# A hand-written order of 968 operations, changed: Pool's list begins with loads, DVE clears the sinks' value tile, and each engine's operations move by a few places

## The chip, the core and the metric

The kernel runs on one core of one Trainium2 chip. A core has five engines that run side by side and wait for each other by semaphores: PE (TensorE, matrix multiply), ACT (ScalarE), DVE (VectorE), POOL (GpSimd) and SP (SyncE, which here only issues DMAs). Sixteen DMA engines move data. POOL's DMAs go through one queue, SP's and ACT's through others. The metric is the time of one launch in device microseconds; less is better.

## The reference

Attention with a sliding window and a few sink keys, then a two-layer perceptron with a sigmoid-gated middle:

```python
q, k, v: (4, 8, 768, 64)      # batch, heads, positions, head width
scores = q @ k.T / sqrt(64)
keep = (pos_k < 4) | ((0 <= pos_q - pos_k) & (pos_q - pos_k < 128))
a = softmax(where(keep, scores, -1e9))
x = (a @ v) as (3072, 512)    # tokens x (heads * width)
h = x @ w_in                  # w_in (512, 2048)
g = h * 1 / (1 + exp(-1.702 * h))
out = g @ w_out               # w_out (2048, 512)
```

## The kernel before

**Tiles.** The 4 x 768 query positions are cut into 24 blocks of 128. Block b is position b % 6 of batch b // 6. A block needs the keys and values of itself and of the block before it in its batch, and the four sink keys of the batch. Blocks 0, 6, 12 and 18 begin a batch and need only themselves; they are done first, then 1, 2, 3, 4, 5, 7 and so on.

**One block's steps, by their names in the code:**
- `q`, `k`, `v` (lines 271, 310, 318): Pool issues a DMA that loads a block and converts it to 16 bits. 128 KB each. Pool also issues the eight weight loads `wi0..3` and `wo0..3` (lines 324 and 331, 512 KB each).
- `tq`, `tk` (383): PE transposes q and k of the first eight blocks through PSUM; `cq`, `ck` are the copies out of it, on ACT or DVE. Later blocks are transposed in pairs by a DMA that SP issues, `tqk` (429).
- `msk` (464), `sc` (478, 483): PE writes the mask and the scores. `snk` (507) are the scores of the sinks.
- `pk`, `mx`, `ms`, `sb`, `ssb` (535 to 596, DVE): the window's two triangles are packed into one tile, the row maximum taken and subtracted; blocks 0, 6, 12 and 18 have `nb` in place of the subtraction.
- `bx`, `ex` (568, 606, ACT): the exponential.
- `ta` (650, PE) with its copy `ca`, or from the seventh block on `tat` (681, a DMA transpose that SP issues): the weights are transposed into tile `at`.
- `sp`, `so` (637, POOL): two selects split the packed triangles again into `atp` (previous block) and `at` (own block).
- `av` (705 to 712, PE): the product with the values, in two halves `av7_0`, `av7_1`. The first matmul (705) adds the sinks through the tile `vsb`; the others are 710 and 712.
- `nm` (722, 723, DVE): division by the sum, into `xn`. `tx` and `cx` (740), or the DMA transpose `txd` (753): `xn` transposed into `xT`.

**The perceptron.** Groups of one or two blocks: g0 is block 0, g1 block 6, g2 blocks 12 and 18, then pairs. `h7_3` is step 3 of the first layer of group 7 (786, PE), `th` and `g` are its gate (800, 807, 816), `o9_1` is step 1 of the four of the second layer for block 9 (836, PE), `ev` the copy out of PSUM (245 on ACT, 239 and 241 on DVE), `st` the store that SP issues (856). A group's first-layer steps use `xT` of all its blocks.

**The sinks' value tile.** `vsa` holds the sink values of each batch (four small DMAs on SP, line 339), with ones beside them. `vsb` (128 x 2080 elements of 16 bits) must be zero but for 32 rows; operation `zv` (228) clears it, and `vsb0..3` (344) write into it the product of `vsa` and an owner mask `own`, one batch each.

**The order.** All operations are recorded in a list of 968; each has an engine or a choice of engines. The string `ORDER` names all of them by number, and a letter after a number (d, a, p, s) chooses DVE, ACT, POOL or SP where there is a choice. They are emitted in that order, so an engine's instruction list is the subsequence of its own operations, and each engine works its list strictly in order. `Plan.emit` asserts that an operation comes behind all that it needs; waits between engines are put in from data and buffers by the framework. Buffers come from rings (three PSUM tiles tagged `mm` for all transposes and both layers, two for scores, four output tiles), so that a buffer's next user waits for its last one. Pool's DMAs use eight completion semaphores in turn: the ninth load is issued only when the first has landed, and so on. Loads of later blocks also depend on the selects of the block six places earlier (line 766).

```python
z_v = plan.add("zv", {DVE: 0.65, POOL: 1.8}, 0,
    lambda e: (nc.vector if e == DVE else nc.gpsimd).memset(vsb, 0.0), key=-880)
for word in order.split():
    choice = letter.get(word[-1])
    op = self.ops[int(word[:-1] if choice else word)]
    op.emit(choice) if len(op.eng) > 1 else op.emit()
```

Of the kernel before, what the change touches and what calls it, by code (L numbers as in the profile page):

```python
# [52 lines left out]


ORDER = """
1a 9 4s 10 11 8p 100 12 2a 7 6 13 0a 94 5a 98 3a 15 96 14 23 107 17 21 101d 26 104 95d 105a 20 102 99d 29 103a 171 97d
108 18 172a 125 106 16 109 150 126a 112 19 194 151a 110 195a 113 148 27 111 149d 225 24 226d 127 114 88 115 152 128d
92 116a 130 129 90 117 119 131 118a 120 86 196 132 121 173 87 197a 122 174a 22 133 135 123 134 199 175 89 124d 138 136
200 25 137 613 139d 30 142 614 153 143 140 615 154 141a 91 619 155 158 144 620 156 145 157 159 621 146 93 616 147d 160
637 617 634 638 618 32 176 639 635 631 636 177 632 610 178 36 633 161 611 179 35 181 628 162a 612 180 163 182 165 622  # L60
164d 166 183 184 33 167 623 185d 629 168 28 198 630 188 204 34 169 640 201 170a 205 227 641 228a 189 39 186 206 624
187a 202 209 230 642 231 203 215 190 38 207 643 208 216d 191 210 217 229 644a 43 192 235 645 211 193a 625 232 31 212a
236 280 37 282 626a 256 233 258 283a 627 652 41 259a 281d 234 257a 649 213 653 238 237 40 261 241 661 650 654 214 239
262 260 651 42 662 285 242 263 304 240 655 218 243a 286 663 44 219 656 646 266 45 657 658 647 220 244 664 648 659 46
267 670 665 245 660 221 671 264 222 246 672 247a 269 265 248 250 268 667 249 666 270 284 251 49 676 668 271 290 47 669
252 677 287 48 253 323 673 288 254 674a 678 291 255a 675 289 306 223 679 292 224a 293 682 307 272 294 680d 305 683 681
688 273 311 295 308 684 50 312 689 686 51 685 309 692 52 313 687 310 276 693 690 314 277 315 704 344 324 345 705 330
691 316 327 325 694 326 331 274 695 296 696 275 361 328 698 697 297 332 278 699 279a 329 53 298 333 334 343 54 299 700
346 317 349 300 701 347 55 335 706 301 702a 318 350 302 703 707 303a 348 57 716 351 399 708a 58 352 362 353 56 709 319
365 717 712 354 368 336 720 320 713 321 337 722 721 322 714 59 723 363 61 718 715 364 366 60 340 719 710 369 724 367  # L70
711 371 370 726 725 341 372 732 338 733 355 339 381 342 382 356 384 727 387 734 64 373 383 388 728 63 385 419 735 62
389 359 736a 390 729 386 737 360 391 750 374 730d 742 392 751 375 752 731 401 67 400 743 402 738 753 406 65 403 378 66
739 746 407 379 748 747 404 376 749 740 408 377 744 741 405 357 409 745 420 358 410 754 393 423 380 426 439 760 440
394 421 755 411 422 68 424 761 427 70 457 756 425 69 762 429 428 757 430 412 766 758d 431 438 413 767 772 444 759 441
72 397 763 445 773 73 442 768 764a 71 398 770 765 769 443 495 416 446 771 788 447 417 448 780 414 458 415 432 774 461
781 449 464 459 433 789 460 462 395 775 74 778 396 75 776 465 418 779 76 463 436 777 782 466 437 790 467 468 783 791
450 784 792d 469 451 434 785 435 78 793 802 786a 514 79 800 803 77 454 798 787 455 470 801 476 799 794 482 471 479 452
795 808 453 80 796 456 809 81 477 806 797 478 82 480 804 807 483 474 805 816 481 475 810 484 497 817 485 498 486 496
516 502 818 499 811 487 503 822 500 552 812 504 823 501 819 505 517 813 820d 506 488 472 821 814d 824 473 489 815 836
825 507 535 83 515 536 828 518 85 837 521 492 84 829 834 519 493 826 835 522 490 827 508 830 520 491 832 831 509 523  # L80
494 844 524 833 525 534 845 590 537 540 838 538 526 846 541 839 539 542 864 543 544 840 512 865 545 527 553 513 847
556 528 559 573 841 848a 574 849 510 842a 852 511 843 546 860 853 529 861 547 850 530 854 851 554 866 855 555 557 531
856 532 560 858 533 857 558 867 859 562 561 550 872 563 551 862 592 868 593 863 564 591 873 597 594 548 880 598 595
869 881 599 565 888 870a 600 596 874 871 889 566 549 601 886 875 567 876d 572 887 602 568 882 575 569 877 578 883 884
570 892 579 571 885 576 878 893 603 580 890 879 581 577 604 894 891 582 900 895 912 583 901 913 607 902 608 896 910
584 897 911 916 585 898a 605 899 917 914 606 918 915 908 919 586 909 906 587 903 907 588 904a 922 589 905 920 609 923
921 928 924 929 925 930 926a 948 927 931 949 938 932a 940 933 939 936 941 946 937 934 947 942 935 950 943 956 944 957
945 951 958 952 962 953 963 954a 959 964 955 960a 965 961 966a 967
"""


# [807 lines left out]
```

## Time and profile before

| | |
|---|---|
| median of three runs | 234.69 us (233.06 to 235.38) |
| the profiled execution, its own time | 235.79 us |
| its span, first to last instruction | 234.10 us |
| granted TensorE clock | 1.00 throughout |
| DMA moved | 32.07 MB, mean 137 GB/s |
| Pool's DMA queue, share of 16 engines' time | 71.9% |
| the queue of SP's and ACT's DMAs | 39.7% |

Durations below come from the profiled execution, which ran 1.1 us longer than the median. PE rows are single matmuls or merged ones, and their ends are modelled. PEld is PE's loading of weights, which runs beside the matmuls. In an instruction's row the bracket at the end gives how long the engine stood idle before it and what ended that.

### The profile page before, as it was taken

The page shows a single profiled execution, that of the slowest core. Times are in us where ns is not written, and L with a number is a line of the kernel's source. Part 1 is how long each engine was busy: PE and PEld are TensorE (multiplying, and loading weights), DVE is VectorE, ACT ScalarE, POOL GpSimd, SP SyncE. Part 2 cuts the span into 40 slices and gives each one's busy share as a digit, 9 for nine tenths or more (in the row PEclk, how much of TensorE's full clock was granted, in tenths as well). Part 3 has the DMA queues.
Part 4 walks back from the last instruction along what each step waited for, and adds up shares of the span by engine and source line. Part 5 has one row for each costly group of instructions (what it writes and reads, how often), then busy time and mean ns, then how long its engine had stood idle before and what let it go on. Part 6 is the DMA issues. An engine that isn't in the chain of part 4 may idle for free.

```text
span 234.1 us, 5451 instructions
## 1 busy us (share of the span) xinstructions
PE 217.5 (93%) x2202; PEld 151.3 (65%) x2202; DVE 150.2 (64%) x384; ACT 143.6 (61%) x224; POOL 111.7 (48%) x129
## 2 busy tenths in 40 slices
PE   1588889999999998979999989999999999999994
PEld 0476765685586585567577567576577676675863
DVE  3478688899978858859787427779647883120000
ACT  2387774874498686266378564697566687552632
POOL 8884344995378729449187294083340303300000
PEclk9999999999999999999999999999999999999999
DMA  3999999999999999999999999999632343313202
GB/s 53 180 159 206 201 196 185 180 170 111 150 226 149 145 219 111 114 234 118 171 221 125 173 171 178 120 194 131 120 115 48 69 97 72 68 42 78 92 0 90
DMA packets 120904, 32.07 MB, mean 137 GB/s; under 512 B 112016, under 2 KB 117936, under 8 KB 120880
## 3 DMA queue, kind: packets, MB, share of 16 engines
q0 software_dynamic: 69888, 13.64, 71.9%
q1 hardware_dynamic: 50272, 17.96, 39.7%
q8 instruction: 17, 0.28, 0.5%
q10 hardware_dynamic: 720, 0.13, 0.3%
q14 instruction: 7, 0.06, 0.1%
HBM read 27.46 MB, written 6.29 MB: 144 GB/s over the span
## 4 chain that ended last, share of the span: by engine, by line
PE 67%; DMA 22%; DVE 5%; POOL 4%; issue 1%; ACT 1%; SPq 0%; POOLq 0%
PE o L836 29%; PE hT L786 27%; DMA w_out<-in_moe_w_out_dram 7%; DMA at<-a 6%; PE sc L483 3%; DMA xT<-xn 3%; DMA v<-in_v_dram 3%; DMA qkn<-in_k_dram 2%; PE av L710 2%; PE av L712 2%; PE av L705 1%; DVE sc L535 1%; POOL at L637 1%; POOL atp L637 1%; DVE mx L545 1%; POOL vsb L228 1%
## 5 line engine op out<-in xcount | busy, mean ns | idle before, releaser
L786 PE MATMUL hT<-xT,w_in 128*128 128x256 f16 (+1 forms) x832 | 94.0, 264 | 1.9 <-DMA xT<-xn 0.9
L836 PE MATMUL o<-w_out,gT 128*128 128x512 f16 (+2 forms) x400 | 92.6, 371 | 0.7 <-DMA w_out<-in_moe_w_out_dram 0.7
L786 PEld LDWEIGHTS <-w_in 128*128 128x128 f16 x832 | 73.8, 98 | 15.9 <-issue 3.7
L816 ACT ACTIVATE gT<-hT 128x512 f16<-128x512 f32 x80 | 46.1, 597 | 28.8 <-PE hT L786 28.3
L637 POOL TENSOR_SCALAR_AFFINE_SELECT atp<-at 128x1024 f16<-128x1024 f16 (+1 forms) x22 | 22.4, 1017 | 74.6 <-DMA at<-a 61.2
L836 PEld LDWEIGHTS <-gT 128*128 128x128 f16 x400 | 35.8, 97 | 33.2 <-issue 2.2
L545 DVE TENSOR_REDUCE mx<-sc 128x4 f32<-128x512 f32 x48 | 32.6, 683 | 1.7 <-PE sc L478 1.7
L535 DVE COPY_PREDICATED sc<-later,sc 128x512 f32<-128x512 uint16 x40 | 26.0, 691 | 7.4 <-PE sc L483 7.1
L606 ACT ACTIVATE a<-e 128x1056 f16<-128x1056 f32 (+2 forms) x24 | 22.3, 935 | 8.7 <-issue 5.8
L582 DVE TENSOR_TENSOR e<-sc,mx 128x512 f32<-128x512 f32 x40 | 26.5, 682 | 0.0
L722 DVE RECIPROCAL rcp<-av 128x4 f32<-128x4 f32 x48 | 8.5, 177 | 24.9 <-PE av L712 24.0
L637 POOL TENSOR_SCALAR_AFFINE_SELECT at<-at 128x1024 f16<-128x1024 f16 (+1 forms) x22 | 22.4, 1017 | 1.2
L271 POOL DMA_DIRECT2D v<-in_v_dram x24 | 21.6, 900 | 1.9 <-DMA qkn<-in_k_dram 0.8
L723 DVE TENSOR_TENSOR xn<-av,rcp 128x256 f16<-128x256 f32 x48 | 20.4, 425 | 1.7
L816 ACT ACT_TABLE_LOAD x13 | 16.7, 1283 | 5.1 <-PE hT L786 4.9
L710 PE MATMUL av<-v,at 128*128 128x65 f16 x192 | 17.4, 194 | 2.0 <-POOL at L637 1.9
L245 ACT COPY osb<-o 128x512 f32<-128x512 f32 (+2 forms) x15 | 8.4, 557 | 16.7 <-PE o L836 16.6
L318 POOL DMA_DIRECT2D qkn<-in_q_dram x18 | 16.1, 893 | 4.5 <-DMA w_out<-in_moe_w_out_dram 4.5
L606 ACT ACT_TABLE_LOAD x12 | 15.4, 1283 | 4.2 <-DVE e L596 2.7
L318 POOL DMA_DIRECT2D qkn<-in_k_dram x18 | 16.1, 893 | 3.6 <-DMA w_in<-in_moe_w_in_dram 1.8
L710 PEld LDWEIGHTS <-at 128*128 128x128 f16 x192 | 14.3, 98 | 5.2 <-POOL at L637 2.4
L712 PE MATMUL av<-v,atp 128*128 128x65 f16 x160 | 15.1, 194 | 0.0
(58 smaller groups left out, 195.1 us busy)
## 6 DMA issues: line engine op xcount, KB each, us to landing
out_dram<-osb SPq DMA_DIRECT2D x23, 256.0 KB, 2.5
qkn<-in_q_dram POOLq DMA_DIRECT2D x24, 128.0 KB, 6.1
qkn<-in_k_dram POOLq DMA_DIRECT2D x24, 128.0 KB, 6.2
v<-in_v_dram POOLq DMA_DIRECT2D x24, 128.0 KB, 6.9
w_in<-in_moe_w_in_dram POOLq DMA_DIRECT2D x4, 512.0 KB, 10.6
w_out<-in_moe_w_out_dram POOLq DMA_DIRECT2D x4, 512.0 KB, 15.4
at<-a SPq DMA_TRANSPOSE x18, 4.5
qkT<-qkn SPq DMA_TRANSPOSE x10, 7.7
```

Of the source, the lines that this page charges most:

```text
L271: f"v{b}", POOL, 0.88, lambda b=b, view=view: nc.gpsimd.dma_start(v65[:, b, :, 0:D], view),
L318: lambda buf=buf, n=n, w=w, view=view: nc.gpsimd.dma_start(buf()[:, n, "qk".index(w)], view),
L535: nc.vector.copy_predicated(out=t()[:, :, :, own].rearrange("p l j s -> p (l j) s"), mask=later.unsqueeze(1).to_broadcast((P, 4, P)), data ...
L545: nc.vector.tensor_reduce(out=part, in_=t()[:, :, :, own], axis=AX.X, op=ALU.max)
L582: nc.vector.tensor_tensor(out=e32()[:, 512 * hf : 512 * hf + 512].rearrange("p (l j s) -> p l j s", l=2, j=2), in0=t()[:, :, :, own], in1= ...
L606: nc.scalar.activation(out=a16()[:, lo:hi], in_=e32()[:, lo:hi], func=AF.Exp, scale=scale)
L637: nc.gpsimd.affine_select(out=dst, in_=at()[:, lo : lo + num], pattern=[[0, num], [1 if own else -1, P]], compare_op=ALU.is_ge if own else ...
L710: nc.tensor.matmul(av()[:, i], at()[:, c], v65[:, b, h], start=(r == 0), stop=(r == 0))
L723: nc.vector.tensor_tensor(out=xn()[:, xi, 4 * hf : 4 * hf + 4].rearrange("p (j l) d -> p l j d", l=2), in0=av()[:, :, 0:D].rearrange("p (l ...
L786: nc.tensor.matmul(ht()[:, n].rearrange("p (n t) -> p n t", n=NT), w_in16[:, c, bass.ts(f, P)], t0()[:, i0 : i0 + NT, c], start=(c == 0), ...
L816: lambda fs=fs, gt=gt, ht=ht: nc.scalar.activation(out=gt()[:, fs[0] : fs[-1] + 1], in_=ht(), func=AF.Gelu_apprx_sigmoid),
L836: nc.tensor.matmul(po()[:, 0:width], gt()[:, F, bass.ts(t, P)], w_out16[:, F, c0 : c0 + width], start=(F == 0), stop=(F == NF - 1),)
```

## The change

Nothing but the string `ORDER` is changed: all 968 operations are there as before. Its first line, before and after:

```diff
-1a 9 4s 10 11 8p 100 12 2a 7 6 13 0a 94 5a 98 3a 15 96 14 23 107 17 21 101d 26 104 95d 105a 20 102 99d 29 103a 171 97d
+1a 9 6 8d 100 15 4a 5a 11 14 7 96 0a 23 94 21 3s 98 17 2s 29 18 104 107 105a 101p 102 103d 16 108 171 20 109 150 19
...
```

`8p` is `zv` on POOL, `8d` on DVE; `101p` is `vsb3` on POOL. What the new string means for each engine's list:

**POOL** (first items)

```
before: zv q0 k0 k18 k6 q12 k1 k12 k2 q6 v0 v6 q1 q18 wi1 wi3 wi2 wi0 wo0 v12 wo1 v18 q2 wo2 wo3
after:  q0 k0 k18 q12 k6 k2 q6 vsb3 v0 k12 v6 q18 k1 q1 wi1 wi3 wi2 v12 wi0 wo0 wo1 q2 v18 wo2 wo3
```

Further on, loads move against selects:

```
before: so5 q13 v13 k13 sp7 so7 k14 v14 q14 sp8 so8 v15 q15 k15 sp9 so9 v16 k16 q16 sp10 so10
after:  so5 q11 v11 q13 sp7 so7 k14 q14 sp8 so8 v15 k13 k15 v14 sp9 so9 v16 q16 k16 q15 sp10 so10 v13
before: sp13 so13 k20 q20 v20 sp14 so14
after:  sp13 so13 v19 sp14 q20 k20 so14 sp15 so15 v20
```

**DVE** begins `zs zk zv za1 z1 ck0 mx0_0 za0 vsb0 nb0_0 mx0_1 vsb2` in place of `zs za0 za1 za2 z1 zk za3 vsb3 vsb0 vsb2 vsb1 ks0 mx0_0`.

**ACT** issues the constants `ident own identb bias0` in place of `ident bias1 bias0 identb later`. **SP** issues `vsa3 vsa1 vsa0 later vsa2 bias1` in place of `own vsa3 vsa0 vsa2 vsa1`. Further on in SP's list:

```
before: tqk9 tat7 st1_ tqk11 st2_ tat8 txd7 tat9 tqk13 st4_ tat10 st3_ txd9
after:  tqk9 st18_ tat7 st6_ tat8 st2_ tqk11 st1_ txd7 tat9 tqk13 tat10 txd9
```

**PE**, the parts that the prediction speaks of:

```
before: h4_6 h4_2 snk9 h4_4 av7_1        h5_6 h5_2 h5_7 snk11 sc11 h5_0 av9_1
after:  h4_7 snk9 h4_2 h4_1 h4_6 av7_1   h5_6 sc11 h5_5 h5_2 h5_7 h5_1 av9_1
before: o5_3 h6_0 sc14 h6_3 av10_1 o7_3  (after: av8_0 h5_4 sc13 snk14 o5_0 snk13 o7_0 av10_1 o5_1)
before: o9_3 o8_2 av13_0 o8_3 h7_4 h7_3 av14_1 h7_2 sc16
after:  o8_2 av13_0 o8_3 sc16 o9_3 h7_3 av14_1 h7_2
```

**Engine of small copies.** `ck0`, `ck6`, `ca6_1` go from ACT to DVE and `cq6`, `ck12`, `cx0` from DVE to ACT. Of the output copies `ev4`, `ev8`, `ev13`, `ev15`, `ev20`, `ev23` go from ACT to DVE, and `ev9`, `ev11`, `ev16` from DVE to ACT.

More of the change, by code (lines that the diff above doesn't have):

```diff
@@ L55 @@
 ORDER = """
-1a 9 4s 10 11 8p 100 12 2a 7 6 13 0a 94 5a 98 3a 15 96 14 23 107 17 21 101d 26 104 95d 105a 20 102 99d 29 103a 171 97d
[L57 to L85, printed above, removed]
@@ L86 @@
-584 897 911 916 585 898a 605 899 917 914 606 918 915 908 919 586 909 906 587 903 907 588 904a 922 589 905 920 609 923
-921 928 924 929 925 930 926a 948 927 931 949 938 932a 940 933 939 936 941 946 937 934 947 942 935 950 943 956 944 957
-945 951 958 952 962 953 963 954a 959 964 955 960a 965 961 966a 967
+1a 9 6 8d 100 15 4a 5a 11 14 7 96 0a 23 94 21 3s 98 17 2s 29 18 104 107 105a 101p 102 103d 16 108 171 20 109 150 19
+172a 10 95d 125 110 24 112 225 111 99d 26 151a 113 126d 27 114 115 97d 88 127 106 128a 130 92 226d 116a 117 12 90 129
@@ new lines @@
+148 118a 119 13 131 149a 22 120 194 132 121 86 196 195a 135 173 197a 87 133 122 134 89 123 199 124a 200 138 30 136 613
+139d 137 25 152 142 174a 140 143 153 614 141d 615 154 91 144 155 619 156 145 157 158 146 616 93 620 147d 159 160 621
+637 32 617 634 638 618 176 639 635 631 36 175 636 177 632 610 178 633 161 611 181 35 628 162a 179 612 180 163 182 165
+622 164d 166 629 184 183 33 167 623 185d 168 39 198 630 169 31 204 640 170a 205 188 227 189 641 228a 201 28 230 186
+206 642 231 209 202 624 187a 203 215 190 38 643 208 191 207 229 216d 210 644a 192 217 235 211 43 193a 625 232 212a 236
@@ new lines @@
+41 280 282 626a 256 281d 258 213 283a 627 233 652 259a 214 237 257a 649 653 218 238 234 261 661 241 40 650 262 654 239
+285 37 260 651 662 242 286 304 44 655 266 243a 263 34 219 656 646 663 42 657 658 647 244 220 664 648 659 245 267 670
+45 665 660 240 221 671 264 268 246 672 247a 269 265 248 667 222 270 249 666 250 284 668 271 251 48 676 669 46 290 252
+323 673 47 253 287 677 291 254 306 272 678 288 255a 674a 223 292 679 273 224a 293 289 682 680d 294 51 307 305 683 50
+688 295 308 311 49 686 309 675 52 684 687 312 689 692 310 685 313 276 693 690 314 277 296 315 704 297 344 324 345 705
@@ new lines @@
+327 691 316 53 330 325 694 326 361 331 274 695 696 275 328 698 697 681 332 278 317 699 279a 333 329 298 334 318 343
+299 700 346 54 347 300 706 55 349 335 701 57 301 350 302 645 319 303a 707 348 702a 352 351 716 708a 320 353 362 336
+321 717 354 720 322 337 365 724 709 59 721 363 399 714 364 368 60 712 715 703 369 725 722 366 713 340 355 723 710 341
+367 718 711 356 371 370 338 719 732 64 339 372 726 342 56 733 62 382 381 373 61 383 727 387 384 359 734 360 385 728
+388 401 735 390 386 729 374 419 389 750 402 391 375 730d 400 736d 751 748 392 67 406 403 742 66 404 752 65 743 407 749
@@ new lines @@
+740 63 753 378 738 379 408 376 739 744 377 393 409 357 405 745 746 358 741 394 420 380 747 439 58 410 754 440 423 421
+760 422 426 397 755 427 411 398 761 424 457 756 425 762 428 757 429 430 412 766 758d 438 759 413 767 763 431 444 69
+441 770 737 442 71 768 771 445 72 764a 772 769 446 68 416 443 773 780 432 447 417 788 781 433 448 414 774 415 73 458
+459 789 775 460 449 464 395 778 396 461 776 418 779 465 782 777 462 436 495 450 783 463 466 790 75 765 437 731 784 467
+74 468 434 451 785 435 476 791 482 786d 800 792a 479 454 793 801 798 469 455 794 514 452 795 802 453 808 803 456 477
@@ new lines @@
+804 809 478 470 799 483 796 480 471 806 797 485 805 484 816 76 481 810 77 486 474 80 496 475 817 70 502 807 499 487
+497 82 811 498 78 500 818 503 81 516 822 504 819 823 505 517 501 812 820a 506 515 821 824 488 518 813 489 825 507 828
+814d 83 472 826 552 473 79 519 832 827 521 829 535 836 833 536 522 492 837 834 508 523 830 524 493 509 520 844 831 84
+835 490 534 525 491 845 540 494 541 838 537 846 526 542 839 538 512 787 847 513 543 840 539 544 553 852 848a 545 527
+573 864 853 574 590 528 510 841 511 865 559 860 842d 529 546 861 556 862 530 850 547 554 854 851 555 85 560 531 855
@@ new lines @@
+856 532 557 858 533 857 561 866 859 558 550 815 562 591 563 551 872 597 867 863 592 564 873 593 598 868 843 594 548
+849 880 595 869 596 881 600 565 888 599 549 874 889 870d 566 601 886 875 884 876a 602 567 885 572 568 878 877 575 569
+879 892 570 578 882 571 893 603 576 887 890 579 604 894 891 577 883 900 580 581 895 582 901 607 912 608 583 896 913
+605 871 897 606 902 898a 910 584 916 911 585 914 917 918 915 908 919 906 909 586 907 903 587 922 588 920 589 923 609
+921 904a 928 924 929 925 930 926d 946 931 947 934 942 935 932a 948 943 933 940 905 927 936 941 899 938 937 949 944 939
@@ L89 @@
+956 945 950 957 951 958 952 962 953 963 954a 959 964 955 960d 965 961 966d 967
 """
```

## The prediction

> **What bounds the kernel now.** I read the page's first lines, then the busy time by stretch of time, then the chain of work that ended last, then the waits of each engine.
>
> ```profile
> span 234.1 us, 5451 instructions
> PE 217.5 (93%) x2202; PEld 151.3 (65%) x2202; DVE 150.2 (64%) x384; ACT 143.6 (61%) x224; POOL 111.7 (48%) x129
> ```
>
> The matrix engine (PE) works 217.5 of 234.1 us and the change takes no matmul away, so only PE's 16.6 us of idle time can be won. The stretches say where it lies (start:end, length, then busy time of PE, PEld, DVE, ACT and POOL):
>
> ```profile
> 0.00:5.00 5.00, 0.50 (x3) 0.38 (x4) 2.19 (x9) 1.27 (x1) 4.40 (x9) 1.00 0.26 40
> 5.00:10.00 5.00, 2.25 (x51) 1.50 (x49) 1.74 (x4) 1.18 (x3) 4.15 (x8) 1.00 1.18 172
> ...
> 80.00:90.00 10.00, 9.33 (x106) 7.42 (x104) 7.06 (x18) 6.92 (x11) 3.99 (x5) 1.00 1.51 179
> ...
> 100.00:110.00 10.00, 8.81 (x107) 7.34 (x105) 7.15 (x18) 6.05 (x10) 7.30 (x8) 1.00 1.41 197
> ...
> 130.00:140.00 10.00, 9.12 (x78) 5.81 (x77) 2.92 (x9) 5.81 (x7) 6.72 (x7) 1.00 1.40 175
> ...
> 220.00:230.00 10.00, 10.00 (x77) 7.10 (x76) 0.00 (x0) 3.76 (x7) 0.00 (x0) 1.00 0.02 7
> 230.00:234.10 4.10, 1.05 (x11) 0.75 (x9) 0.00 (x0) 0.93 (x3) 0.00 (x0) 1.00 0.36 128
> ```
>
> Idle at the start: 4.50 + 2.75 = 7.25 us in the first ten. In the middle three holes: 0.67, 1.19 and 0.88, 2.74 together. At the end 3.05, the last eviction and store, which stay. The chain tells what fills the start (start us, us, what):
>
> ```profile
> 0.80 1.83 POOL vsb L228
> ...
> 3.94 5.59 DMA qkn<-in_k_dram
> ...
> 17.60 16.59 DMA w_out<-in_moe_w_out_dram
> 34.23 1.02 PE o L836 x4
> ```
>
> It begins with Pool's clearing of the sinks' value tile and then runs through Pool's loads alone until 34.23. PE's timeline confirms that it waits for weights in that stretch:
>
> ```profile
> 22.59 1.07 PE L786 MATMUL hT<-xT,w_in 128*128 128x128 f16 x16 [0.35 <-DMA w_in<-in_moe_w_in_dram]
> 25.14 2.85 PE L786 MATMUL hT<-xT,w_in 128*128 128x128 f16 x48 [0.34 <-DMA w_in<-in_moe_w_in_dram]
> 34.23 1.02 PE L836 MATMUL o<-w_out,gT 128*128 128x512 f16 x4 [0.66 <-DMA w_out<-in_moe_w_out_dram]
> ```
>
> So until 34.23 the time is set by when Pool's stream of loads began and how fast it flows. Two weight loads of the same size land 25.14 - 22.59 = 2.55 us apart: the stream flows at a rate of its own, not at Pool's pace of issue, about 0.6 us for a load.
>
> **The front.** Before, Pool clears 2080 columns first and issues its first load after that:
>
> ```profile
> 2.58 0.78 POOL L310 DMA_DIRECT2D qkn<-in_q_dram  x1
> 3.34 1.79 POOL L310 DMA_DIRECT2D qkn<-in_k_dram  x3
> ...
> 9.81 0.90 POOL L271 DMA_DIRECT2D v<-in_v_dram  x1 [0.85 <-DMA qkn<-in_k_dram]
> ```
>
> Now the first load can be issued at 0.80, which is 2.58 - 0.80 = 1.78 us earlier. Thirteen loads stand ahead of the first weight load in both lists, and ahead of the second w_out load stand the same loads in both (v12 has moved up past wi0 and wo0, but wo1 was behind it before as well). So the landings that PE waited for at 22.59, 25.14 and 34.23 all come 1.78 earlier: **-1.78**. wi0 and wo0 come one v load later against the rest, about 1 us; PE's three waits for weights are those quoted, none of them for these two.
>
> ```profile
> 3.46 1.36 DVE L344 TENSOR_TENSOR vsb<-vsa,ownm 32x520 f16<-32x520 f32 x2 [1.07 <-DMA vsa<-in_v_dram]
> ```
>
> What could eat this? Pool takes over one of four multiplications by the owner mask (vsb3), eighth in its list. No row shows it on Pool. DVE needs 0.68 us for one; Pool cleared 2080 columns in 1.83, so 520 are at least 0.46; and Pool's selects of 1024 columns take about 1.09, which I take as the upper end. I take 1.0, nearest to the select, which also reads and writes SBUF. It delays the eighth issue, but seven loads are then in the queue (k18 was issued at 3.94 and landed 5.59 later, at 9.53), so the queue doesn't run dry, and Pool's own wait of 0.85 before the tenth load covers most of it. vsb3 waits for two constants and for DVE's clearing. DVE's cost:
>
> ```profile
> L231 DVE MEMSET a<- 128x64 uint32 x4 | 0.4, 112 | 0.0
> L229 DVE MEMSET vsa<- 32x260 f32 x1 | 0.3, 275 | 0.9 <-PEq L880 0.9
> L241 DVE COPY osb<-o 128x512 f32<-128x512 f32 x6 | 4.1, 692 | 4.4 <-PE o L836 4.3
> ```
>
> From 64 to 260 elements a clearing grows from 112 to 275 ns, 0.83 ns each; 1040 words of four bytes make 0.92 us. With the other early memsets DVE is done near 2.6, before any q or k has landed: **0**, hidden by the first load's landing. If that cover went, 0.92.
>
> Does DVE's early work slow Pool's issues? Beside DVE's two mask products at 3.46 Pool issued three loads in 1.79 us, 0.60 each: not stretched. [...]
>
> Two of the small constants now go out while the loads already flow:
>
> ```profile
> identb<-cidentb ACTq DMA_DIRECT2D x1, 32.0 KB, 2.1
> later<-clater ACTq DMA_DIRECT2D x1, 32.0 KB, 4.1
> ```
>
> The mask that was issued last took 4.1 us instead of 2.1. If bias0 and identb now take 4.1, the first scores come up to 2 us later than they could, and block 0's chain gains nothing; PE still catches up in its waits of 0.35, 0.34 and 0.66, so this costs at most 1.78 - 1.35 = 0.4 of the front. I take 0 and keep 0.4.
>
> **The middle.** The three holes are these, with the work that was late, and the prices of one step on PE:
>
> ```profile
> 78.53 7.86 DMA at<-a
> ...
> 95.19 7.25 DMA at<-a
> ...
> 116.38 0.87 PE hT L786 x8
> 117.25 0.54 PE sc L483 x8
> ...
> 127.76 7.84 DMA xT<-xn
> ```
>
> ```profile
> PE av L710 <- POOL at L637: 1.9, 2, 1.2
> PE hT L786 <- DMA xT<-xn: 0.9, 1, 0.9
> ```
>
> Each hole ends a transposition by DMA of 7.3 to 7.9 us. They are slow ones:
>
> ```profile
> qkn<-in_k_dram POOLq DMA_DIRECT2D x24, 128.0 KB, 6.2
> at<-a SPq DMA_TRANSPOSE x18, 4.5
> ```
>
> First hole (0.67, block 7): PE's list has the same work ahead of av7_1 (h4_7 for h4_4). Two loads, v13 and k13, move behind block 7's selects, and tqk11 behind tat8, so less runs beside the slow transposition; by the median it could be 3.4 us shorter. That the loads slow it is an inference, so I count **0** and keep -0.67. Second hole (1.19, block 9): one more first-layer step stands ahead of av9_1 (h5_5 and h5_1 for h5_0), **-0.87**. Third hole (0.88, group 7): sc16 (0.54) moves ahead of the group's first step, and the loads k20, q20 and v20, issued just ahead of that transposition, move behind block 14's first select. Together I count the whole hole, **-0.88**; bounds -0.54 and -0.88. The table loads on ACT are as many as before. The last evictions go to DVE, which is idle there (0.00 busy from 220 on): DVE copies 512 columns in 0.69, so 192 cost about 0.26 against ACT's 0.32: **0**.
>
> ```profile
> 231.09 0.32 ACT osb L245
> ```
>
> **Sum.** -1.78 - 0.87 - 0.88 = -3.5 us. On the profiled execution, 235.79 us with a span of 234.1, that is 232.3. That run was 1.1 above the median of 234.69, from which I count: **231.2 us**. With all three holes gone 230.5; with only half of the middle's gain 232.1.
>
> **Rivals.** *The attention chain doesn't follow.* If the transpositions and loads between 45 and 150 us are bound by the DMA engines (share 1.4 to 1.5 in the rows above), blocks 7 to 14 become ready no more than 1.78 earlier, and each hole that a filler closes opens at the next tight product. Then 234.69 - 1.78 = 232.9. For it: the slow transpositions. Against: loads have been moved out of their way. Chance 0.20.
>
> *The front is eaten.* [...] Chance 0.10.
>
> *Slower: SP's queue behind k13.* k13 now waits behind both selects of blocks 7 and 8, and tat10 stands directly behind tqk13, which needs k13, while av10_1 has lost cover on PE: h6_0, h6_3, five second-layer steps and sc14 no longer stand ahead of it, 2 x 0.87 + 5 x 0.86 + 0.54 = 6.6 us.
>
> ```profile
> 92.53 1.09 POOL L637 TENSOR_SCALAR_AFFINE_SELECT at<-at 128x1024 f16<-128x1024 f16 x1
> ...
> 108.59 1.09 POOL L637 TENSOR_SCALAR_AFFINE_SELECT at<-at 128x1024 f16<-128x1024 f16 x1
> ```
>
> ```profile
> 97.48 4.42 SPq L429 DMA_TRANSPOSE qkT<-qkn  x1
> ...
> 102.69 1.30 SPq L681 DMA_TRANSPOSE at<-a  x1
> ```
>
> ```profile
> 118.61 0.27 PE L705 MATMUL av<-vsb,at 128*128 128x260 f16 x1
> ```
>
> PE now reaches av10_1 at 118.61 - 6.6 - 3.5 = 108.5; its select ends at 108.59 + 1.09 - 1.78 = 107.9. Cover 0.6 instead of 8.9. k13 is issued after block 8's selects and v15, near 93.62 + 0.9 - 1.78 = 92.7, and with 6.2 lands at 98.9, 3.2 after tqk13 would start (95.7). If SP's 4.42 for tqk13 is work, av10_1 is 2.6 late; if the transposition behind it is as slow as the three above (3.4 over the median), 6.0: 231.2 + 6.0 = 237.2. If the 4.42 is mostly waiting for the transposition ahead, as I believe, since SP needs 1.30 for tat10 itself, nothing is lost. It decides from a lateness of 0.6, and turns the sign from 4.1. Chance 0.15, with whatever else a new order may block.
>
> **Chances and range.** Forecast 0.55, rivals 0.20, 0.10, 0.15. About 1%, 2.3 us, is what a measurement of this kernel can tell from no change. The forecast lies below 232.3 and counts as faster; the first two rivals lie within 1%; the third is slower. The forecast's own range is 229.8 (all holes gone, 230.5, and 0.7 for the scatter of runs) to 232.3; reaching up over the two middle cases it ends at 235.2, leaving out the slow case and a little below.
>
> **What would show it.** First load issued near 0.8 and no clearing at the head of the chain; PE's wait for w_out ending near 32.4 instead of 34.23; waits for "POOL at L637" down from 1.9 to about 1.0 and none on xT; a span near 230.6. It is wrong if the w_out wait ends later than 33.3 (front eaten), if new waits on transposed blocks over 1 us stand between 85 and 150 us, or if a product of block 10 waits on Pool.

## The result and the profile after

Timed beside the kernel before on one chip, the changed kernel took 232.62 us (median of 14 runs, 231.87 to 233.41), the kernel before 235.03 us (14 runs, 233.06 to 240.53). The ratio is 0.993 with a 95% interval of 0.991 to 0.996, a gain of about 1.6 us. The ratio leaves out runs that took over 1.5% longer than the fastest of their kernel, five of the fourteen of the kernel before and none of the changed one, so it shows less than the 2.4 us between the medians. Timed a second time, the ratio was 0.992 (0.989 to 0.996). The forecast was 231.2, a gain of 3.5 us or 1.5%; a gain of 0.7% lies within the 1% that the prediction took as the least that can be told, though the interval does not reach 1.

The profiled execution of the changed kernel took 232.43 us; 235.79 before. First the head of its page and then the waits of PE (engine, line, what it waited for: us in total, times, longest):

```profile
span 230.7 us, 5431 instructions
PE 217.0 (94%) x2202; PEld 151.6 (66%) x2202; DVE 154.5 (67%) x388; ACT 139.8 (61%) x220; POOL 111.2 (48%) x129
```

```profile
PE tq L383 <- DMA qkn<-in_q_dram: 5.7, 1, 5.7
PE ta L650 <- ACT qkT L245: 1.2, 1, 1.2
PE tx L740 <- DVE xn L723: 1.0, 2, 0.6
PE sc L478 <- DVE qkT L241: 0.8, 1, 0.8
PE hT L786 <- ACT gT L816: 0.5, 1, 0.5
PE hT L786 <- DMA xT<-xn: 0.3, 1, 0.3
```

PE's busy time is 0.5 us less than before, and the span is 3.4 us shorter: 2.9 of that is idle time. The waits for w_in, w_out and Pool's selects are gone. A wait of 0.3 for a transposed block (`xT`) is left; it stands at 97.52, not in the third hole's place (135.64 before). New are the waits of block 0's own chain (lines 650 and 478) and 0.5 in the middle. The stretches, with the columns of the prediction, show the same; the 10 us from 80, 100 and 130 on, which had the three holes, are full:

```profile
0.00:5.00 5.00, 0.00 (x0) 0.00 (x0) 1.57 (x5) 1.28 (x1) 3.89 (x11) 1.00 0.44 57
5.00:10.00 5.00, 3.25 (x62) 2.44 (x64) 1.29 (x2) 0.58 (x1) 4.99 (x8) 1.00 1.36 182
80.00:90.00 10.00, 10.00 (x110) 8.14 (x108) 8.19 (x21) 7.70 (x13) 7.15 (x8) 1.00 1.61 211
90.00:100.00 10.00, 9.66 (x78) 5.43 (x77) 7.76 (x20) 4.54 (x5) 2.89 (x4) 1.00 1.64 144
100.00:110.00 10.00, 10.00 (x113) 7.39 (x112) 8.18 (x22) 6.74 (x10) 8.24 (x9) 1.00 1.34 134
130.00:140.00 10.00, 10.00 (x107) 7.91 (x104) 6.33 (x15) 7.51 (x11) 2.97 (x4) 1.00 1.14 176
140.00:150.00 10.00, 9.45 (x77) 5.20 (x75) 7.62 (x21) 7.09 (x9) 5.77 (x7) 1.00 1.72 123
```

The front did not start where it was forecast. Pool's timeline of the changed kernel (start, length, engine, line, operation; in brackets the idle time before):

```profile
1.32 0.78 POOL L310 DMA_DIRECT2D qkn<-in_q_dram  x1 [0.81 <-POOLq L880]
2.08 1.20 POOL L310 DMA_DIRECT2D qkn<-in_k_dram  x2
...
5.63 1.23 POOL L344 TENSOR_TENSOR vsb<-vsa,ownm 32x520 f16<-32x520 f32 x1
...
8.27 0.97 POOL L271 DMA_DIRECT2D v<-in_v_dram  x1
```

The first load is issued at 1.32. That is 1.26 earlier than before, not 1.78, though Pool had nothing to do from 0.5 on. PE's timeline shows the products that waited for weights before, at 22.59, 25.14 and 34.23:

```profile
20.04 1.05 PE L786 MATMUL hT<-xT,w_in 128*128 128x128 f16 x16 [0.24 <-ACT xT L245]
...
22.42 1.06 PE L786 MATMUL hT<-xT,w_in 128*128 128x128 f16 x16
...
24.35 2.84 PE L786 MATMUL hT<-xT,w_in 128*128 128x128 f16 x48
```

None of them waits for a load now. The third comes 0.79 earlier than before, and the first product with w_out's second part came at 32.91 instead of 34.23, 1.32 earlier. The first product with w_in, however, stayed where it was: 20.04, and 19.99 before.

### The profile page after: what moved, and what is told of

The parts are those of the page before. It is cut to its first block, busy times and chain, and to the rows that moved or that the text cites. A ratio compares the mean times of both kernels' runs of the same rounds, so it can differ in the third digit from the quotient of the medians.

```text
span 230.7 us, 5431 instructions
## 1 busy us (share of the span) xinstructions
PE 217.0 (94%) x2202; PEld 151.6 (66%) x2202; DVE 154.5 (67%) x388; ACT 139.8 (61%) x220; POOL 111.2 (48%) x129
## 5 line engine op out<-in xcount | busy, mean ns | idle before, releaser
L836 PEld LDWEIGHTS <-gT 128*128 128x128 f16 x400 | 36.1, 98 | 33.3 <-issue 1.9
L535 DVE COPY_PREDICATED sc<-later,sc 128x512 f32<-128x512 uint16 x40 | 26.8, 689 | 3.6 <-PE sc L483 3.3
L241 DVE COPY osb<-o 128x512 f32<-128x512 f32 (+2 forms) x10 | 6.3, 634 | 21.2 <-PE o L836 21.1
```

What stands on the lines that cost most here:

```text
L535: nc.vector.copy_predicated(out=t()[:, :, :, own].rearrange("p l j s -> p (l j) s"), mask=later.unsqueeze(1).to_broadcast((P, 4, P)), data ...
L836: nc.tensor.matmul(po()[:, 0:width], gt()[:, F, bass.ts(t, P)], w_out16[:, F, c0 : c0 + width], start=(F == 0), stop=(F == NF - 1),)
```

## The experiments

Two theories stood against each other at first. By mine, the steps of the sum were about right for the one execution that was profiled, and wrong for the median: the holes of the middle vary from execution to execution, and I took their size in a slow one off the median. By the rival, the holes belong to the order and are always there, and what was lost is the front or something that took the holes' place.

### The kernel before, five more profiles

No edit. In the table below these are repeats 1 to 5.

> The kernel before, unchanged, profiled again. If the three holes of the middle (0.67, 1.19 and 0.88 us in the first profile, whose time of 235.79 us lay 1.1 above the median) vary from execution to execution, a look whose time lies near 234 shows them smaller in sum, by about what it is faster, and the front (first load at 2.58, third key-and-value product at 25.14, first product with w_out at 34.23) stays where it was. If the holes belong to the order of the operations, they stand here with sizes within 0.3 us of the first profile, and the difference between times lies elsewhere (in the granted clock or in the front).

> As the first look: by the theory that the holes vary, their sum follows the time of the execution with a slope near 1; by the rival they stay within 0.3 us of 0.67, 1.19 and 0.88 whatever the time.

> As the first two looks. With four profiles of this kernel, the smallest and the largest sum of the three holes should differ by over 1.5 us by the theory that they vary, and by under 0.6 us by the rival.

> The kernel before once more. In four profiles of it (232.99, 234.83, 235.79 and 238.64 us) the PE's idle time between 80 and 150 us was 0.80, 1.63, 2.73 and 2.83 us, and the slowest had in addition a stretch of lower granted clock. By the theory that these waits make the scatter, this look's idle time lies between those of the two profiles between whose times its own time lies, within 0.5 us, where the granted clock is full. By the rival that the front makes it, the idle time there is 1 to 2 us whatever the time, and the first product with w_out moves with the time (33.22 in the fastest, 34.23 in the first).

> As the look before this one: idle time of the PE between 80 and 150 us follows the time by the one theory, and the start of the first product with w_out by the other.

All profiles of the study in one table: the time of that execution, the start of the first product with w_out's second part, the start of the first half product of block 1 with its values, and PE's idle time between 80 and 150 us (70 minus its busy time there). A star marks a profile with a drop of the granted clock.

| kernel | time | w_out product | block 1 | idle 80 to 150 |
|---|---|---|---|---|
| before, first profile | 235.79 | 34.23 | 49.88 | 2.73 |
| before, repeat 1 | 232.99 | 33.22 | 48.98 | 0.80 |
| before, repeat 2 | 234.83 | 33.63 | 49.88 | 1.63 |
| before, repeat 3 * | 238.64 | 33.90 | 49.91 | 2.83 |
| before, repeat 4 | 234.90 | 33.21 | 49.00 | 2.59 |
| before, repeat 5 | 234.74 | 33.68 | 49.58 | 1.93 |
| changed | 232.43 | 32.91 | 48.30 | 0.95 |
| changed, again | 232.64 | 32.61 | 47.98 | 1.43 |
| changed, Pool clears | 234.00 | 34.57 | 49.94 | 0.59 |
| changed, block 0 first | 231.91 | 32.44 | 47.82 | 0.44 |
| changed, small clearing first * | 233.98 | 34.52 | 49.90 | 0.67 |
| before, DVE clears * | 235.17 | 34.26 | 49.88 | 2.07 |
| before, new Pool and SP lists | 234.84 | 32.63 | 48.57 | 1.08 |
| changed, old Pool and SP lists | 236.52 | 33.68 | 49.45 | 3.18 |

The rows behind the last column, for the fastest execution of the kernel before (repeat 1) and for repeat 4, in the view of stretches:

```profile
80.00:115.00 35.00, 34.50 (x325) 23.52 (x324) 25.57 (x67) 21.04 (x28) 19.24 (x21) 1.00 1.49 165
115.00:150.00 35.00, 34.70 (x324) 23.59 (x325) 24.25 (x64) 23.28 (x30) 19.65 (x21) 1.00 1.47 166
```

```profile
80.00:115.00 35.00, 33.08 (x314) 22.48 (x312) 25.91 (x66) 20.31 (x28) 19.13 (x20) 1.00 1.47 160
115.00:150.00 35.00, 34.33 (x326) 23.63 (x325) 23.65 (x60) 22.10 (x29) 19.14 (x20) 1.00 1.60 164
```

The same program has 0.5 + 0.3 us of idle time there in one execution and 1.92 + 0.67 in another. So the holes do vary, by 2.0 us between the extremes, and the rival that they stand within 0.3 us falls. Repeats 4 and 5 lie where the theory put them (2.59 between 1.63 and 2.73; 1.93 against at most 1.63 + 0.5). The expected slope near 1 is missed: between repeats 1 and 2 the time differs by 1.84 and the idle time there by 0.83. The front, which I expected to stand still, varies too, from 33.21 to 34.23, but does not order the times: repeats 1 and 4 have the same front and differ by 1.9 us. The mean of the six is 2.09 us between 80 and 150; the profile that the forecast was read from had 2.73, the second largest, and its product with w_out was the latest of the six (mean 33.65).

One by one, the three holes vary more than their sum shows. These are all their rows with a wait over 0.15 us in the five repeats: one of repeat 2, two of repeat 4, two of repeat 5.

```profile
103.94 0.20 PE L710 MATMUL av<-v,at 128*128 128x65 f16 x1 [0.96 <-POOL at L637]
...
88.01 0.20 PE L710 MATMUL av<-v,at 128*128 128x65 f16 x1 [0.73 <-POOL at L637]
104.06 0.20 PE L710 MATMUL av<-v,at 128*128 128x65 f16 x1 [1.19 <-POOL at L637]
...
88.25 0.20 PE L710 MATMUL av<-v,at 128*128 128x65 f16 x1 [0.38 <-POOL at L637]
104.02 0.20 PE L710 MATMUL av<-v,at 128*128 128x65 f16 x1 [0.91 <-POOL at L637]
```

With the first profile, the first hole (0.67 there) stands in three of six profiles, the second (1.19) in four, and the third (0.88) in the first profile alone. The means over the six are 0.30, 0.71 and 0.15 us. Repeats 1 and 3 have none of the three; repeat 3, the slowest, waits elsewhere.

### The clearing alone

The kernel before with one letter changed:

```diff
-1a 9 4s 10 11 8p 100 12 2a 7 6 13 ...
+1a 9 4s 10 11 8d 100 12 2a 7 6 13 ...
```

> The kernel before, with its first Pool operation, the clearing of the sinks' value tile, given to DVE and nothing else moved. By the theory that the front is worth what the profile after shows (first load issued at 1.32 instead of 2.58, first product with w_out 1.3 us earlier) this gives 1.3 us of the 1.6 measured for the whole change: a ratio near 0.9945, a median near 233; the three holes of the middle remain as they were, 0.5 to 2.7 us in sum. By the rival that the weights land earlier but the middle gives it back (its waits on copies and transfers grow by what the products come earlier), the ratio is 0.998 to 1.002 and the holes in the profile grow by about 1.3 us in sum. By the prediction's own sum it would be 1.78 us, a ratio of 0.992.

Measured: 234.16 us (12 runs, 231.87 to 236.67) beside 234.75; ratio 0.996 (0.992 to 1.000), about 1.0 us, between the first theory's 1.3 and the rival's nothing, which the interval just reaches. The middle kept its holes (2.07), and they did not grow. Not everything came earlier by as much as the issue did: the first load left 1.26 earlier and the second and third products with w_in, which still wait for their loads, came 1.14 and 0.78 earlier (21.45 and 24.36), but the constant `identb` landed at 6.59 instead of 4.45, and the mask's product waited for it:

```profile
PE sc L464 <- DMA identb<-cidentb: 6.6, 1, 6.6
PE av L710 <- POOL at L637: 1.7, 2, 0.9
PE hT L786 <- DMA w_in<-in_moe_w_in_dram: 1.1, 2, 0.7
```

What this one profile gained at the start it lost at 24 us to the clock; that is told at the end.

### The new order with the clearing on Pool, and the changed kernel again

The changed kernel with `8p` in place of `8d`, and, timed beside it, the changed kernel itself:

```diff
-1a 9 6 8d 100 15 4a 5a 11 14 7 96 ...
+1a 9 6 8p 100 15 4a 5a 11 14 7 96 ...
```

> The changed kernel with the clearing of the sinks' value tile back on Pool, ahead of its first load, and all else as changed. By the theory that both parts of the change are worth something, it loses the front alone: first load issued near 2.6, first product with w_out 0.2 to 1.3 us later than in the changed kernel, and 0.2 to 1.3 us slower than that (a ratio of 0.994 to 0.999 to the kernel before). By the rival that all of the gain is the front, it is no faster than the kernel before (0.999 to 1.003). By the rival that all of it is the middle, it is as fast as the changed kernel (0.992 to 0.994).

> The changed kernel, unchanged, timed and profiled again. By the theory that the new order of the middle has taken away holes whose size varied from execution to execution, its times scatter less than those of the kernel before beside it (first comparison: 231.87 to 233.41 against 233.06 to 240.53), its profile again shows no wait over 0.6 us on the PE between 80 and 150 us and a first product with w_out near 32.9, and the ratio is again near 0.993. By the rival that the small scatter of its first comparison was chance, the profile shows waits over 0.6 us on the transposed blocks or on Pool between 80 and 150 us and times above 235.

Measured: 234.13 us with Pool clearing (12 runs, 233.22 to 235.49), 232.95 for the changed kernel (8 runs, 232.44 to 234.05), 235.17 for the kernel before (24 runs, 232.90 to 237.68). By the medians the front is worth 234.13 - 232.95 = 1.2 us, and the new order without it 235.17 - 234.13 = 1.0. By the ratios to the kernel before (0.999 with 0.996 to 1.002, and 0.992) the split is 1.6 and 0.3 us: the times alone cannot tell the middle's part from nothing, and the rival that all of the gain is the front is not excluded by them. The profiles speak for the middle: the five that keep all of its new order have 0.44 to 1.43 us of idle time between 80 and 150 (mean 0.82), the six of the kernel before 0.80 to 2.83 (mean 2.09). Nor is this kernel the kernel before with a new middle alone. The first load left at 2.58 and the product with w_out came at 34.57, 2.0 after that of the changed kernel timed beside it (1.3 was the most expected) and 0.9 after the mean of the kernel before. The two kernels with the new middle scatter over 1.6 and 2.3 us, the kernel before over 4.8. The changed kernel's second profile has no wait on Pool, but 0.8 us on `xT`, so the bound of 0.6 that I had set was missed there.

### Half of the new middle at a time

The kernel before with the new Pool list (behind the last w_out load) and SP list; and the changed kernel with the old ones. Part of Pool's list, old and new:

```diff
-so5 q13 v13 k13 sp7 so7 k14 v14 q14 sp8 so8 v15 q15 k15 sp9 so9
+so5 q11 v11 q13 sp7 so7 k14 q14 sp8 so8 v15 k13 k15 v14 sp9 so9
```

> The kernel before with the changed kernel's order on Pool behind the last w_out load and on SP, and with its own order on PE, DVE and ACT and its own front. If the places of the loads and transpositions are what made the holes of the middle, they go here: waits of the PE between 80 and 150 us of 1 us in sum (0.8 to 2.8 in the four profiles of the kernel before), times within about 2 us of one another, and the level of the changed kernel with the clearing on Pool (234.1). If it is the order of the PE's work that covers them, they stay: 0.8 to 2.8 us, times over a range of 4 us and more, and a median near that of the kernel before beside it.

> The changed kernel, its front included, with Pool's order behind the last w_out load and SP's order as in the kernel before: PE, DVE and ACT work in the changed order. If the order of the PE's work is what covers the holes, this is as fast and as even as the changed kernel (about 232.9, within 2 us of one another). If the places of the loads and transpositions matter, it has the front's gain alone (about 1.2 us under the kernel before) and waits of the PE between 80 and 150 us of 1.5 to 3 us.

Measured beside 235.30 of the kernel before: new Pool and SP lists alone 235.05 us (233.40 to 238.70), ratio 1.002 (0.998 to 1.006); new PE, DVE and ACT lists with the new front alone 235.42 us (233.76 to 238.46), ratio 1.003 (0.998 to 1.009). Neither expectation came true as a whole: the idle time came out about as in the theory that the movers' places matter (1.08 with the new Pool and SP lists, 3.18 with the old ones), but neither half is worth anything by itself, the second not even with the front in it.

What the lists of Pool and SP do is seen at block 7, whose first select waits for the transposition of its weights to land. That took 6.3 to 7.9 us in the six profiles of the kernel before. With the new lists in that kernel SP issues it at 77.26 and the select begins at 82.50, at most 5.2 us later; in the changed kernel it is 77.20 and 82.71, at most 5.5 us; with the old lists in the changed kernel the transposition took 8.1. So the movers' places do shorten this one, whichever order PE has. For the paired transpositions of q and k this is not shown: the traces show the landings of a few of them only, and the eighth of the ten took 8.3 to 9.7 us in the kernel before, but 4.6 in either half.

With the new Pool and SP lists, then, the idle time between 80 and 150 falls to 1.08. But the old order on PE meets a slow transposition further on. Waits of PE in that kernel, and its timeline:

```profile
PE hT L786 <- DMA xT<-xn: 1.6, 1, 1.6
```

```profile
165.00 1.05 PE L786 MATMUL hT<-xT,w_in 128*128 128x256 f16 x8 [1.57 <-DMA xT<-xn]
```

The transposition that this group waits for was issued at 158.16 and took 6.80 us to land, against 3.2 to 4.8 for the same one in the six profiles of the kernel before. In the changed kernel the group's first product starts at 165.46, 0.5 later, without a wait. In the other half PE reaches block 7's product at 87.90, 0.25 earlier than in the first profile, while block 7's selects end 0.77 later; and 35 us on, a division (`xn`) comes 1.26 late. Its PE and Pool timelines, and after them Pool's in the changed kernel:

```profile
89.59 0.20 PE L710 MATMUL av<-v,at 128*128 128x65 f16 x1 [1.69 <-POOL at L637]
...
124.91 0.29 PE L705 MATMUL av<-vsb,at 128*128 128x260 f16 x1 [1.26 <-DVE xn L723]
```

```profile
87.29 1.09 POOL L637 TENSOR_SCALAR_AFFINE_SELECT atp<-at 128x1024 f16<-128x1024 f16 x1 [6.87 <-DMA at<-a]
```

```profile
82.71 1.09 POOL L637 TENSOR_SCALAR_AFFINE_SELECT atp<-at 128x1024 f16<-128x1024 f16 x1 [2.99 <-DMA at<-a]
```

Block 7's select begins at 87.29 behind the old lists and at 82.71 behind the new. The halves need one another: whole, the change gains 0.8%, and either half gains nothing. The likely reason is that the movers make transpositions early and the order on PE, DVE and ACT is made for those times. That the new waits are what each half loses is read from one profile of each.

### Pool's first load behind a small clearing

```diff
+    spare = const.tile([P, 64], FP16, name="spare")
+    nc.gpsimd.memset(spare, 0.0)
```

> The changed kernel with one small clearing of a spare tile of 128 x 64 elements put on Pool ahead of its first load; nothing reads it. In the changed kernel the first load was issued at 1.32, 0.52 us after the 0.80 at which Pool's clearing had begun in the kernel before, and behind an idle time of 0.81 put down to Pool's own sequencer. If Pool's first transfer has a fixed earliest start near 1.3, the small clearing (0.1 to 0.4 us from 0.80 on) fits ahead of it and the first load still is issued at 1.3 to 1.4. If what came late is whatever stands first in the list, or the transfer needs those 0.5 us after whatever precedes it, the first load is issued at 1.7 or later.

Measured: 233.98 us, one run, with a drop of the clock at 18 us (told at the end), so that its time says nothing here. Pool's timeline:

```profile
0.81 0.15 POOL L864 MEMSET spare<- 128x64 f16 x1 [0.29 <-POOLq L882]
1.35 0.78 POOL L310 DMA_DIRECT2D qkn<-in_q_dram  x1 [0.39 <-issue]
```

The clearing runs at 0.81, where the first load was forecast, and the load still goes out at 1.35. A clearing that stands first on Pool starts at 0.80 in the kernel before and at 0.81 here, while Pool's first transfer, where it stands first, is issued at 1.32 (the changed kernel, and the kernel before with DVE clearing), and 0.15 us of other work ahead of it delays it by 0.03. What holds the transfer until then, the traces do not show.

### Block 0's chain first

PE's transposes of block 0's keys and weights move up. On DVE `vsb0` and `vsb1` move ahead of `ck0`, and `vsb2` behind `ck6`. Part of the order, before and after:

```diff
-172a 10 95d 125 110 24 112 225 111 99d 26 151a 113 126d 27 114 115 97d ...
+103d 108 171 109 150 172a 125 110 112 111 151a 113 126d 99d 114 115 225 ...
```

> The changed kernel with the first block's chain brought forward: on PE the transposes of its first keys stand ahead of its scores' mask and those of its first weights ahead of the third block's keys; on DVE three of the operations that build the sinks' value tile stand ahead of the eviction of the first keys and the last one behind that of the seventh. In the changed kernel the first product of keys and values with the first block's weights started at 20.04, as in the kernel before (19.99), though the loads came 1.3 us earlier: if that chain, not the landing of the weights, now sets the front, this brings that product to about 19 and the first product with w_out from 32.91 to about 32.3, and saves 0.6 us of the changed kernel's time. By the rival that the landings of w_in and w_out set it (23.76 and 32.23 in the changed kernel), nothing moves behind 25 us and the time is the changed kernel's.

Measured: 232.75 us (11 runs, 231.91 to 233.70) beside 232.95 of the changed kernel; ratio to the kernel before 0.991 (0.987 to 0.994). The two can't be told apart; the expected 0.6 us is not seen. The chain moved as meant, the w_out product too (32.44), and the span of its profile was 230.2 against 230.7 and 230.9:

```profile
18.88 1.05 PE L786 MATMUL hT<-xT,w_in 128*128 128x128 f16 x16 [0.24 <-ACT xT L245]
...
23.37 2.85 PE L786 MATMUL hT<-xT,w_in 128*128 128x128 f16 x48
```

The third product with w_in began at 23.37, and the load it needs had landed at 23.32: with the chain 1.1 us earlier, the landings bind again. So chain and landings lie within about 1 us of one another, and neither alone is worth much more.

## Why the prediction missed

**The sum, step by step.** It said 235.79 → 232.3 for the profiled execution, and the changed kernel's profiled execution took 232.43. That this agrees is partly luck, for errors of both signs cancel: the front came 0.46 short and 0.9 us of new waits in the middle were not in the sum, while the first hole (0.67), counted at nothing, and 0.32 more of the second went as well. The steps that failed:

- *"The front. -1.78."* Its direction held: nothing else queues ahead of the weights, and PE no longer waits for them. The size was off, for two reasons. The sum rested on the first load at 0.80, where Pool's clearing had begun; the load went out at 1.32, 1.26 earlier than before, and so it does behind a small clearing too. And once the loads came earlier, they no longer set PE's pace: the third product with w_in came only 0.79 earlier, because block 0's own chain, whose first product with w_in stayed at 20.04, had gained nothing (with block 0's chain moved up, these two products come at 23.37 and 18.88). The prediction named this case, priced it at 0.4 and counted it at 0. Taken against the mean of six profiles of the kernel before (33.65), the product with w_out came 0.9 earlier in the changed kernel's two (32.91 and 32.61); by the medians with and without the clearing on Pool the front is worth 1.2.
- *"Together I count the whole hole, -0.88."* The third hole stands in the first profile alone. The second and third together are 0.71 + 0.15 = 0.86 us on the mean of the six, where the sum had 0.87 + 0.88 = 1.75.
- *"That run was 1.1 above the median of 234.69, from which I count."* This is the step that turned 232.3 into 231.2. The run was longer in part because its holes were large: 2.73 us of idle time between 80 and 150, where the six profiles have a mean of 2.09 and the fastest 0.80. To take the holes of a long run off the median is to take a part of them off twice. The changed kernel's median is 232.62, and its own idle time there 0.95 and 1.43, so the middle's share is 2.09 - 1.19 = 0.9 on the mean of its two profiles (1.3 with the three variants that keep its middle), 1.0 by the medians and 0.3 by the ratios with Pool clearing.

That the two shares by the medians, 1.2 + 1.0, make up the whole 235.17 - 232.95 = 2.2 us follows from how they were taken and confirms neither.

**The holes one by one.** In the changed kernel's two profiles none of the three is left. For the second hole this is the forecast; for the third it says little, since five of six profiles of the kernel before lack it too. The first (0.67) was counted at nothing because it was only an inference that loads slow the transposition; the half with the new Pool and SP lists shows that their places shorten the transposition of block 7's weights (at most 5.2 us against 6.3 to 7.9). In exchange there are 0.55 us at 146.38 and 0.3 on `xT`, which the sum did not have.

**Costs counted at nothing.** The clearing on DVE took 0.93 (estimate 0.92) and ended at 2.36, long before the first q landed (5.63). Its row, then the eviction that moved to DVE:

```profile
1.43 0.93 DVE L228 MEMSET vsb<- 128x1040 uint32 x1 [0.17 <-issue]
...
8.22 0.69 DVE L241 CAST qkT<-tk 128x512 f16<-128x512 f32 x1 [4.93 <-PE tk L383]
```

The owner product on Pool took 1.23, above the upper end of 1.09, and was hidden too. Beside the cast at 8.22, which took 0.69, Pool issued its load at 8.27 in 0.97 us, where the same load took 0.90 before: 0.07 more, so DVE's cast did not hold it up for the cast's length.

**The rivals.** SP's queue behind `k13` was forecast to leave block 10 a cover of 0.6. It left 1.3: the second select ended at 106.44 + 1.09 = 107.53 and PE came at 108.87, without a wait. (The 0.6 was too small by its own working: it took the whole 3.5 off PE's time, though the third hole's 0.88 lies behind block 10; without it the cover is 1.5.)

```profile
106.44 1.09 POOL L637 TENSOR_SCALAR_AFFINE_SELECT at<-at 128x1024 f16<-128x1024 f16 x1
```

```profile
108.87 0.27 PE L705 MATMUL av<-vsb,at 128*128 128x260 f16 x1
```

*The attention chain doesn't follow* gave 232.9, close to what was measured, but by luck: its parts are all of a front of 1.78 and nothing of the middle. Its mechanism, a closed hole that opens again at the next tight product, is what both half versions show, in one profile each, and the whole change does not. *The front is eaten*, that the first transfers take longer as they start earlier, is partly right: in the clearing alone `identb` landed 2.1 us later (6.59 against 4.45), and in the changed kernel it took 4.2 us instead of 2.1. The sign to look for, a w_out wait ending later than 33.3, did not appear.

What stays open is which pair of moves makes the two halves of the middle fit; only whole lists were exchanged.

## What to carry to other kernels

A stall that is read from one profiled execution has the size of that execution: take it off that execution's own time, or look at several profiles first, but do not take it off a median that was faster. When operations were moved on several engines together, price them together: each half of this order closed one wait and met another. An estimate of what starts earlier needs the row of the same kind of instruction, not of the one that stood there before (here a clearing at 0.80, a load at 1.32).

## What the hardware showed

**The clock dropped behind waits of 0.7 to 2.1 us.** In three profiles the granted clock fell to 0.50 to 0.63 after waits of PE. Repeat 3 of the kernel before, in stretches of 2 us (the clock is the third number from the end):

```profile
148.00:150.00 2.00, 0.72 (x4) 0.21 (x3) 1.93 (x6) 0.00 (x0) 0.00 (x0) 1.00 1.41 131
150.00:152.00 2.00, 1.19 (x10) 0.97 (x10) 1.29 (x5) 0.08 (x1) 0.04 (x1) 1.00 0.88 193
152.00:154.00 2.00, 2.00 (x7) 0.76 (x5) 0.00 (x0) 1.97 (x3) 1.93 (x2) 0.52 0.79 151
154.00:156.00 2.00, 2.00 (x8) 0.70 (x6) 0.69 (x1) 1.99 (x2) 2.00 (x4) 0.63 0.06 4
```

A wait of 2.08 us was followed by 4 us at 0.52 and 0.63 of the clock, in which a busy PE loses an estimated 2 x 0.48 + 2 x 0.37 = 1.7 us. The same stood at 24 us in the kernel with the clearing alone (0.60 and 0.54, 1.7 us), behind waits of at most 0.7 us, and at 18 us in the one with the small clearing (0.53, 0.50, 0.50, 0.77), behind a wait of 1.56; but not in the changed kernel with the old Pool and SP lists, behind a wait of 1.69 us:

```profile
88.00:90.00 2.00, 0.41 (x10) 0.41 (x11) 0.39 (x1) 0.42 (x1) 1.93 (x3) 1.00 0.95 259
90.00:92.00 2.00, 2.00 (x27) 1.82 (x25) 1.92 (x5) 0.81 (x2) 2.00 (x3) 1.00 0.71 45
```

So the length of a wait alone doesn't decide it: the clock dropped behind waits of at most 0.7 us and stayed at 1.00 behind one of 1.69. What does decide it, the traces do not show.

How often it happens can be told from the mean granted clock of each timed run (0.993 for repeat 3). It is under 0.995 in 28 of 64 runs of the kernel before, timed beside the variants, and in none of 22 of the changed kernel; with the new order and Pool clearing 2 of 12, with block 0 first 1 of 11, with the new Pool and SP lists 4 of 12, with the old ones 3 of 12, with the clearing alone 3 of 12. So the drops are rarer with the whole new order. But they do not explain the old one's scatter: those 28 runs took 235.4 us on the mean, the other 36 235.0, and the fastest of all 64 (232.53) is one of the 28. That is 0.3 us between them, not 1.7; where in those runs the drops fell is not known.

**One transposition took 6.3 to 7.9 us.** That is the time from issue to landing for block 7's weights in six profiles of one and the same program; with the new Pool and SP lists it took at most 5.2 us, in the changed kernel at most 5.5. The 1.6 us between 6.3 and 7.9 are more than a hole of 1 us.
